# A linear-attention and MLP kernel: k's column maxima by way of DRAM instead of TensorE

## The chip, the cores and the metric

The kernel runs on one core of a Trainium2 chip. The metric is the device time of one execution in microseconds (us); the time before is the median of three runs. Beside it stands one profiled execution, from whose trace all rows below are taken.

A core has five engines with an instruction queue each: TensorE (PE in the rows, its weight loads PEld), VectorE (DVE), ScalarE (ACT), GpSimd (POOL) and SyncE (SP), which here only issues DMAs. An instruction waits at the head of its queue until the semaphores that it needs are set, and everything behind it waits too.

## The reference

```python
q_s = softmax over the 64 columns of each row of q          # with the row's maximum subtracted
k_s = k - np.max(k, axis=2, keepdims=True)                  # maximum over the 576 positions
k_s = np.exp(k_s)
k_s = k_s / (np.sum(k_s, axis=2, keepdims=True) + 1e-09)
kv  = np.einsum('bhsd,bhse->bhde', k_s, v)
x   = np.einsum('bhsd,bhde->bhse', q_s, kv)                 # then 4608 rows x 512
h   = x @ w_in                                              # 512 x 2048
g   = 0 where h <= -1, h where h >= 1, else (h + 1)**2 / 4
out = g @ w_out                                             # 2048 x 512
```

There are 8 batches of 8 heads, 576 positions and 64 columns. The step that the change touches is `np.max(k, axis=2)`: for each column of k one maximum over all positions of its head.

## The kernel before, in words

Two heads make a pair, so a batch has 4 pairs with 128 columns each. The 4608 rows of x are cut into 9 chunks of 512 rows. For each chunk the MLP runs 16 times over 128 hidden columns: a first product `h` (line 1446), the activation on ACT and DVE (lines 1596 to 1605), and a second product `o` (line 1659). All operands are split into a high and a low part, so a product is three matmuls of 128x512. Chunks 0 to 2 are done one by one; chunks 3 to 8 go in twos with a scheme of seven products (`hA`, `hb`, `hC`, line 1505) in place of eight.

Between these matmuls stands the attention. For batches 0 and 1 k is loaded transposed (columns on the partitions, `in_kt`), where the maximum is a plain reduction along the row (line 952). For batches 2 to 7 k is loaded with positions on the partitions (128 partitions, 5 positions each, `in_k`), two pairs at a time, in the function `attention_two`. It is called twice for each of the six batches, 12 times in all. There the maximum goes these steps for the two pairs:

- `k_max` (line 1213, DVE): maximum over the 5 positions that one partition holds, read with a stride; 128x128 values per pair, into `m2`.
- `k_tr` (line 1221, PE): a transpose of `m2` into PSUM, bank `a`, one per pair.
- `k_top` (line 1227, DVE): the maximum of each row of the transposed tile, for both pairs, into `mx`.
- `k_spread` (line 1232, PE): a transpose of that column broadcast to 128 columns, so that every partition has all 128 maxima, in PSUM.
- `k_sub` (line 1242, DVE) subtracts it, `k_exp` (line 1248, ACT) takes the exponent, `kv_mms` (line 1258, PE) makes the 20 small matmuls of `kv` for the two pairs, each of which shows as two in the trace.

The order of all instructions is written out before the program is built. The class `Plan` holds every operation with an engine, a duration, a due time and what it depends on. `order`, `late` and `early` make a list of it; `settle` then tries changes, one for each number in the table `TURNS` (a seed of a random choice), and keeps a change where the mean of three plays (`play`) ends no later. So a change of any operation moves instructions on every engine of the whole program. SP has one queue for all DMAs, in that order; a store that waits for its data holds the loads behind it.

A ring (`ring(tag, n)`) stands for n buffers that are used in turn: who takes one waits for the last readers of the one n before it. PSUM bank `a` is such a ring of one, shared by the scaled weights (`sg`, line 603), `mt`, `kv` and half of `x`.

## Time and profile before

| | |
|---|---|
| median of 3 runs | 846.63 us (845.81 to 847.31) |
| profiled execution, its own time | 844.76 us |
| its span from the first to the last instruction | 843.0 us |
| PE busy | 828.4 us, 98% of the span |
| DVE, ACT, POOL busy | 457.3, 442.5, 329.1 us |
| TensorE clock granted | full speed (2.4 GHz) in every slice |
| DMA | 166.38 MB, mean 197 GB/s |

The page sums the whole program. PE is the engine to look at: a gap in it lengthens the run, unless it is made up later. A busy PE is not a PE at its peak, as matmuls overlap, so what a piece of PE work costs is read from the distance of the starts around it, not from its duration.

### The profile page before, as it was taken

How to read it: one execution, taken by the hardware profiler on the slowest of the kernel's cores; microseconds unless marked ns; L12 is line 12 of the kernel's file. 1: busy time of each engine (PE TensorE's matmuls, PEld its weight loads, DVE VectorE, ACT ScalarE, POOL GpSimd, SP SyncE). 2: the span in 40 equal slices, each digit the busy share in tenths (PEclk: the TensorE clock that was granted, in tenths of full speed). 3: DMA queues.
4: the chain of work that ended last, by engine and by line, in shares of the span. 5: the costliest groups of instructions: out<-in, count | busy, mean ns of one | idle time of the engine just before them, and what ended most of it. 6: DMA issues, size and time to landing. Idle time of an engine off the chain costs nothing.

```text
span 843.0 us, 12228 instructions
## 1 busy us (share of the span) xinstructions
PE 828.4 (98%) x4364; PEld 663.6 (79%) x4364; DVE 457.3 (54%) x853; ACT 442.5 (52%) x758; POOL 329.1 (39%) x291
## 2 busy tenths in 40 slices
PE   8899999999999999999999999999999999999998
PEld 6587778877777787877877888787778888888786
DVE  6887774566756656776754315765641034545300
ACT  6787756443466454644656445554574245444522
POOL 4664555552446756200217691102157600000153
PEclk9999999999999999999999999999999999999999
DMA  9898865457578566766675536556465254544232
GB/s 338 274 318 294 290 218 213 145 165 241 193 258 274 173 217 224 246 215 228 194 248 206 153 99 194 195 193 210 145 216 178 76 187 138 175 138 162 75 102 87
DMA packets 65580, 166.38 MB, mean 197 GB/s; under 512 B 7280, under 2 KB 7536, under 8 KB 65520
## 3 DMA queue, kind: packets, MB, share of 16 engines
q1 hardware_dynamic: 65520, 165.61, 58.7%
q8 instruction: 34, 0.56, 0.3%
q14 instruction: 26, 0.21, 0.1%
HBM read 122.06 MB, written 43.52 MB: 196 GB/s over the span
## 4 chain that ended last, share of the span: by engine, by line
PE 93%; DVE 2%; ACT 2%; issue 1%; POOL 1%; DMA 1%; POOLq 0%; ACTq 0%
PE o L1659 45%; PE h L1446 16%; PE hA L1505 15%; PE hC L1505 8%; PE hb L1505 4%; PE x L839 2%; PE kv L1258 2%; PE warm L1841 1%; PE kv L988 1%; DMA out<-osb 1%; DVE qmo L1345 0%; ACT r L1596 0%; PE ep L963 0%; ACT osb L533 0%; PE tp L1035 0%
## 5 line engine op out<-in xcount | busy, mean ns | idle before, releaser
L1659 PE MATMUL o<-wl,gh 128*128 128x512 f32 x576 | 227.8, 396 | 0.3 <-ACT osb L533 0.3
L1659 PE MATMUL o<-wh,gl 128*128 128x512 f32 x576 | 224.9, 390 | 0.1
L1659 PE MATMUL o<-wh,gh 128*128 128x512 f32 x576 | 224.4, 390 | 0.0
L1505 PE MATMUL hA<-x,w 128*128 128x512 f32 x576 | 145.8, 392 | 1.6 <-ACT sn_P L533 1.2
L1659 PEld LDWEIGHTS o<-wl,gh 128*128 128x128 f32 x576 | 108.1, 188 | 26.8 <-issue 3.6
L1659 PEld LDWEIGHTS o<-wh,gl 128*128 128x128 f32 x576 | 108.1, 188 | 24.9 <-POOL gl L1648 1.0
L1505 PEld LDWEIGHTS hA<-x,w 128*128 128x128 f32 x576 | 107.2, 188 | 26.0 <-ACT sn_P L533 1.8
L1659 PEld LDWEIGHTS o<-wh,gh 128*128 128x128 f32 x576 | 108.2, 188 | 21.4
L1446 PE MATMUL h<-x,w 128*128 128x512 f32 x432 | 110.1, 396 | 2.2 <-DVE gl L1648 1.5
L1446 PEld LDWEIGHTS h<-x,w 128*128 128x128 f32 x432 | 79.3, 188 | 23.0 <-DVE gl L1648 2.1
L1600 ACT ACTIVATE r<-r 128x512 f32<-128x512 f32 x139 | 87.8, 633 | 3.8
L1505 PE MATMUL hC<-x,w 128*128 128x512 f32 x288 | 73.9, 392 | 0.1
L1596 ACT ACTIVATE r<-c,half 128x512 f32<-128x512 f32 x48 | 34.7, 723 | 68.2 <-DVE c L1529 68.1
L1648 POOL TENSOR_TENSOR gl<-gs,gh 128x512 fp32r<-128x512 f32 x42 | 54.2, 1291 | 41.7 <-ACT gh L1643 41.1
L1354 POOL TENSOR_TENSOR q<-q,qzb 128x512 f32<-128x512 f32 x28 | 28.9, 1050 | 105.3 <-DVE qzb L1376 91.0
L1354 POOL TENSOR_TENSOR q<-q,qmb 128x512 f32<-128x512 f32 x28 | 28.8, 1049 | 100.9 <-DVE qmb L1346 100.9
L1154 POOL TENSOR_TENSOR x<-xc,x 128x512 fp32r<-128x512 f32 x40 | 51.8, 1307 | 35.9 <-ACT x L1149 35.9
L1643 ACT CAST gh<-gs 128x512 fp32r<-128x512 f32 x42 | 26.1, 622 | 73.2 <-PE o L1659 63.4
L1505 PEld LDWEIGHTS hC<-x,w 128*128 128x128 f32 x288 | 53.6, 188 | 12.3 <-DVE sn_P L535 0.5
L1596 ACT ACTIVATE r<-h,half 128x512 f32<-128x512 f32 x48 | 33.0, 687 | 52.2 <-PE h L1446 51.9
L1648 POOL TENSOR_TENSOR gl<-c,gh 128x512 fp32r<-128x512 f32 x6 | 7.8, 1294 | 126.9 <-ACT gh L1643 126.8
L1605 DVE SCALAR_TENSOR_TENSOR h<-h,r 128x512 f32<-128x512 f32 x48 | 33.1, 694 | 37.1 <-ACT r L1600 34.0
(123 smaller groups left out, 1176.3 us busy)
## 6 DMA issues: line engine op xcount, KB each, us to landing
w<-b SPq DMA_DIRECT2D x50, 512.0 KB, 4.5
w<-s SPq DMA_DIRECT2D x48, 512.0 KB, 3.5
st<-in_w SPq DMA_DIRECT2D x32, 512.0 KB, 6.2
g<-c SPq DMA_DIRECT2D x42, 256.0 KB, 4.1
gs<-g SPq DMA_DIRECT2D x42, 256.0 KB, 2.6
v<-in_v SPq DMA_DIRECT2D x32, 325.0 KB, 4.9
q<-in_q SPq DMA_DIRECT2D x36, 256.0 KB, 3.7
out<-osb SPq DMA_DIRECT2D x35, 256.0 KB, 2.5
```

The lines of the kernel that those rows point to most:

```text
L839: nc.tensor.matmul(t[r][cols, :, p0:p1], kvt[rows, g % NKV, pr, :], q[pr]["tq"][rows, :, p0:p1], start=True, stop=True, tile_position=(r * ...
L1154: eng.tensor_tensor(x[:, 1, :], t["xc"][:, at, :], f32(x[:, 0, :]), ALU.subtract)
L1258: nc.tensor.matmul(kv[d, i, :], t[pr]["k"][:, j, d], t[pr]["v"][:, j, e * (D + 1) : (e + 1) * (D + 1)], start=(j == 0), stop=(j == KJ - 1) ...
L1354: nc.gpsimd.tensor_tensor(qf, qf, at, alu)
L1446: nc.tensor.matmul(t["h"], lhs, rhs, start=(turn == 0 and i == 0), stop=(turn == NPAIR - 1 and i == 2),)
L1505: nc.tensor.matmul(banks[b]["h"], lhs, rhs, start=(begins and not kk and not m), stop=(ends and kk == 1 and m == 2), skip_group_check=True,)
L1596: nc.scalar.activation(t["r"], t["h"], AF.Relu, bias=half[:, :1], scale=0.5)
L1600: nc.scalar.activation(t["r"], t["r"], AF.Square)
L1605: nc.vector.scalar_tensor_tensor(t["h"], t["h"], 1.0, t["r"], ALU.max, ALU.min)
L1643: nc.scalar.copy(t["gh"], t["h"])
L1648: eng.tensor_tensor(t["gl"], t["h"], f32(t["gh"]), ALU.subtract)
L1659: nc.tensor.matmul(outs[c, j], lhs[:, s], rhs, start=(begins and i == 0), stop=(closes and i == 2),)
```

## The change

For batches 2 to 7 the transposed copy of k is now loaded as well (`in_kt` holds all 8 batches, 24 more loads of 288 KB), into the buffers from which k itself follows later. `k_max` is the plain reduction along the row, one column of a fixed tile `kmax` per pair. `m_turn` turns that tile by blocks of 32x32 on DVE, so that the maxima of a pair lie in 4 partitions of 32 values. `m_store` writes them to DRAM, 4 rows of 128 bytes, one DMA per pair; `m_load` reads both pairs' 256 values back to all 128 partitions, one DMA of 128 KB. `k_sub` reads that tile from SBUF. `k_tr`, `k_top` and `k_spread` are gone: 48 transposes on PE, of some 3900 matmul instructions written there before, and 12 reductions on DVE. Chains of this kind run 12 times, as before.

The planner's `play` now adds 0.1 to an operation on PE of another mode than the one before (0 for the big matmuls, 1 for `x`, 2 for `kv`, 3 for transposes), two durations of PE operations are 0.09 and 0.1 lower, and the table `TURNS` is another. The maxima's operations have due times of their own.

```diff
--- before.py
+++ after.py
@@ -91,6 +91,7 @@
         self.store = False
         self.margin = 0.8 if kb else 0.0
         self.wire = kb / 330
+        self.mode = 0
         for d in deps:
             d.users.append(self)
 
@@ -122,76 +123,66 @@
     UNDER_WAY = 8
 
     TURNS = (
-        10001, 10002, 10003, 10011, 10013, 10026, 10029, 10031, 10033, 10036, 10041, 10042,
...
+        6, 9, 10, 15, 19, 20, 25, 27, 30, 31, 37, 39, 41, 42, 43, 44, 45, 46, 47, 49, 57, 58,
...
     )
 
     CASES, LATE = 3, 1.6
@@ -321,6 +312,7 @@
         free = dict.fromkeys(("PE", "ACT", "DVE", "POOL", "SP", "port", "wire"), 0.0)
         last = dict.fromkeys(free)
         ends, gaps, why = {}, [], {}
+        mode = 0
         for op in order:
             e = op.engine
             t, by = free[e], last[e]
@@ -349,6 +341,8 @@
                 gaps.append((op, t - free[e]))
                 if t > free[e] + 3 and t > START:
                     t += 2.4
+            if e == "PE" and op.mode != mode:
+                t, mode = t + 0.1, op.mode
             ends[op] = free[e] = t + op.us
             if op.port:
                 free["port"], last["port"] = ends[op], op
@@ -535,6 +529,7 @@
             nc.vector.tensor_copy(out, src)
 
     half = const.tile([P, 32], F32, name="half")
+    kmax = const.tile([P, 64], F32, name="kmax")
 
     kvt = const.tile([P, NKV, NPAIR, D], F32, name="kvt")
     early = ExitStack()
@@ -878,7 +873,8 @@
         rings_ = [ring(f"ps {tag}", 1) for _, tag in banks]
         deps = [kvdone.get((b, pr)) for b in (c - 1, c) for pr in two]
         deps = [d for d in deps if d] + [d for r in rings_ for d in r.wait()]
-        xm = do("PE", 1.05, due, x_mm, *ready, *deps)
+        xm = do("PE", 0.95, due, x_mm, *ready, *deps)
+        xm.mode = 1
         for i, pr in enumerate(two):
             ring(f"wk t{'ab'[i]}", 2).free(xm)
             kvread[c - 1, pr] = xm
@@ -1050,6 +1046,7 @@
         rrz.take(kz)
         et = ring(f"ps h{pr % 2}", 1) if first else rpk
         tr = do("PE", 0.6, 2, kt_tr, ke, *rpk.wait(), *(et.wait() * first))
+        tr.mode = 3
         rpk.take(tr)
         copies = [("DVE", 0.69, False)], [("ACT", 0.25, False)]
         kc = do("ACT", 0.58, 2.5, kt_copy, tr, *rk.wait(), other=copies[0])
@@ -1057,12 +1054,14 @@
         if not first:
             rpk.free(kc)
             tr = do("PE", 0.25, 2.7, kt_tr2, ke, *rpk.wait())
+            tr.mode = 3
             rk.free(tr)
         et.take(tr)
         kd = do("DVE", 0.25, 2.8, kt_tail, tr, kc, other=copies[1])
         et.free(kd)
         deps = [kc, kd, lv, *(rpk.wait() if not first else [])]
         mm = do("PE", 0.9, 3.5, kv_mm, *deps)
+        mm.mode = 2
         if not first:
             rpk.take(mm)
         rk.free(mm)
@@ -1082,6 +1081,7 @@
         qn = do("POOL", 1.04, 3, q_rows("qrz", ALU.mult), qz, port=True)
         rqz.free(qn)
         tr = do("PE", 0.45, 3.6, q_tr, qn, *rpq.wait())
+        tr.mode = 3
         rpq.take(tr)
         rq.free(tr)
         if first:
@@ -1207,38 +1207,34 @@
 
         def k_max(i):
             def emit():
-                if not i:
-                    b["m"] = wk.tile([P, 2, P], F32, tag="m2", name=f"m2_{n}")
-                k = t[two[i]]["k"].rearrange("p j d -> p d j")
-                nc.vector.tensor_reduce(b["m"][:, i, :], k, AX.X, ALU.max)
-
-            return emit
-
-        def k_tr(i):
-            def emit():
-                if not i:
-                    b["mt"] = ps_a.tile([P, 4, P], F32, tag="a", name=f"mt_{n}")
-                nc.tensor.transpose(b["mt"][:, i, :], b["m"][:, i, :], ident)
-
-            return emit
-
-        def k_top():
-            b["mx"] = sm.tile([P, 32], F32, tag="mx", name=f"mx_{n}", bufs=1)
-            nc.vector.tensor_reduce(b["mx"][:, :2], b["mt"][:, 0:2, :], AX.X, ALU.max)
-
-        def k_spread(i):
-            def emit():
-                t[two[i]]["mb"] = b["mt"][:, 2 + i, :]
-                nc.tensor.transpose(
-                    t[two[i]]["mb"], b["mx"][:, i : i + 1].broadcast_to([P, P]), ident
+                kt_ = t[two[i]]["kt"].rearrange("p j s -> p (j s)")
+                nc.vector.tensor_reduce(kmax[:, i : i + 1], kt_, AX.X, ALU.max)
+
+            return emit
+
+        def m_turn():
+            b["mt"] = sm.tile([P, QB], F32, tag="mt", name=f"mt_{n}", bufs=1)
+            nc.vector.transpose(b["mt"], kmax[:, :QB])
+
+        def m_store(i):
+            def emit():
+                nc.sync.dma_start(
+                    maxima[i].rearrange("(r p) -> r p", p=QB), b["mt"][i : P : QB, :]
                 )
 
             return emit
 
+        def m_load():
+            b["m"] = wk.tile([P, 2, P], F32, tag="m2", name=f"m2_{n}")
+            nc.sync.dma_start(
+                b["m"].rearrange("p i d -> p (i d)"),
+                maxima.rearrange("i p -> (i p)").unsqueeze(0).broadcast_to([P, 2 * P]),
+            )
+
         def k_sub(pr):
             def emit():
                 k = t[pr]["k"]
-                mb = t[pr]["mb"].unsqueeze(1).broadcast_to([P, KJ, P])
+                mb = b["m"][:, pr % 2, :].unsqueeze(1).broadcast_to([P, KJ, P])
                 nc.vector.tensor_tensor(k, k, mb, ALU.subtract)
 
             return emit
@@ -1276,37 +1272,42 @@
             )
 
         if c < NB:
-            rm = ring("wk m2", 1)
-            loads, rooms, maxed = {}, {}, rm.wait()
+            loads, rooms = {}, {}
+            tag = ("k", "st1")[h]
+            maxima = dp.tile([2, P], F32, name=f"mk{n}")
+            rx, ry, rm = ring("sm mx", 1), ring("sm mt", 1), ring("wk m2", 1)
+            tops, before = [], rx.wait()
             for i, pr in enumerate(two):
-                tag = ("k", "st1")[h]
-                loads[pr, "k"], rooms[pr, "k"] = load(
-                    pr, "k", k[c - KT, pr], [P, KJ, P], 320, kdue + 6 * i, tag
+                lk, rk = load(pr, "kt", kt[c, pr], [P, 1, S], 288, kdue - 14 + 3 * i, tag)
+                km = do("DVE", 0.75, kdue - 12 + 3 * i, k_max(i), lk, *before)
+                rk.free(km)
+                tops.append(km)
+                if not i:
+                    rx.take(km)
+                before = [km]
+            turn = do("DVE", 0.15, kdue - 7, m_turn, *tops, *ry.wait(), port=True)
+            rx.free(turn)
+            ry.take(turn)
+            kept = [plan.save(0.45, kdue - 6, m_store(i), [turn], 32) for i in range(2)]
+            ry.free(*kept)
+            spread = plan.read(0.45, kdue - 2, m_load, [*kept, *rm.wait()], 128)
+            rm.take(spread)
+            subs, exps = [], []
+            for i, pr in enumerate(two):
+                lk, rooms[pr, "k"] = load(
+                    pr, "k", k[c - KT, pr], [P, KJ, P], 320, kdue + 10 + 6 * i, tag
                 )
                 loads[pr, "v"], rooms[pr, "v"] = load(
                     pr, "v", v[c, pr], [P, KJ, P + 2], 325, kdue + 33 + 3 * i, "v"
                 )
-            for i, pr in enumerate(two):
-                km = do("DVE", 1.3, kdue + 6 * i, k_max(i), loads[pr, "k"], *maxed, port=True)
-                maxed = [km]
-                if not i:
-                    rm.take(km)
-                loads[pr, "m"] = km
-            exps = []
-            ra = ring("ps a", 1)
-            one = do("PE", 0.13, kdue + 8, k_tr(0), loads[two[0], "m"], *ra.wait())
-            ra.take(one)
-            other = do("PE", 0.13, kdue + 8, k_tr(1), loads[two[1], "m"], one)
-            top = do("DVE", 0.4, kdue + 10, k_top, one, other)
-            rm.free(top)
-            spread = [do("PE", 0.13, kdue + 12, k_spread(i), top) for i in range(2)]
-            subs = [do("DVE", 0.81, kdue + 14, k_sub(pr), *spread) for pr in two]
-            ra.free(*subs)
+                subs.append(do("DVE", 0.9, kdue + 14, k_sub(pr), lk, spread, port=True))
+            rm.free(*subs)
             exps = [do("ACT", 0.74, kdue + 20 + 12 * i, k_exp(pr), subs[i]) for i, pr in enumerate(two)]
             ra = ring("ps a", 1)
             at = kdue + 34
             deps = [loads[pr, "v"] for pr in two]
-            mm = do("PE", 1.34, at, kv_mms, *exps, *deps, *ra.wait())
+            mm = do("PE", 1.25, at, kv_mms, *exps, *deps, *ra.wait())
+            mm.mode = 2
             ra.take(mm)
             for pr in two:
                 rooms[pr, "k"].free(mm)
@@ -1831,6 +1832,7 @@
     stream.__enter__()
     make_identity(nc, ident)
     nc.vector.memset(half, 0.5)
+    nc.gpsimd.memset(kmax, 0.0)
 
     nc.scalar.activation(half[:, 1:2], half[:, :1], AF.Exp)
 
@@ -1869,7 +1871,7 @@
 
     kk = rows(inputs["k"]).transpose(0, 1, 3, 4, 2, 5).reshape(b, NPAIR, P, 2 * KJ * D)
 
-    kt = rows(inputs["k"])[:KT].transpose(0, 1, 2, 5, 4, 3).reshape(KT, NPAIR, P, KJ * P)
+    kt = rows(inputs["k"]).transpose(0, 1, 2, 5, 4, 3).reshape(b, NPAIR, P, KJ * P)
     kt = kt[..., :S]
     kk = kk[KT:]
     vv = rows(inputs["v"], pad=True)
```

How instructions moved is shown at three places. The names give batch (or chunk) and pair (or hidden block), and a buffer number last.

The first is PE at the start: the first two blocks of the first layer (`h_0_0`, `h_0_1`, twelve matmuls each, three per part of x) and the transposes of batch 1's k (`ep`, then `et`, which takes the same bank after DVE has copied `ep` out). Before:

```order
L1446 MATMUL h_0_0_473<-x2_482,w_0_0_454 128x512 x3
L1446 MATMUL h_0_1_501<-x2_482,x10_488 128x512 x3
L1446 MATMUL h_0_0_473<-x3_491,w_0_0_454 128x512 x3
L963 MATMUL ep_1_0_538<-ident_95,k_1_0_410 128x128 x4
L1446 MATMUL h_0_1_501<-x3_491,x10_488 128x512 x3
L972 MATMUL et_1_0_570<-ident_95,k_1_0_410 64x128
L1659 MATMUL o_0_1_572<-wl0_97,gh_0_0_562 128x512
```

After:

```order
L1447 MATMUL h_0_0_498<-x3_502,w_0_0_469 128x512 x3
L1447 MATMUL h_0_1_523<-x1_463,x10_487 128x512 x3
L1447 MATMUL h_0_1_523<-x2_495,x10_487 128x512 x3
L1447 MATMUL h_0_1_523<-x3_502,x10_487 128x512 x3
L959 MATMUL ep_1_0_557<-ident_96,k_1_0_419 128x128 x4
L968 MATMUL et_1_0_581<-ident_96,k_1_0_419 64x128
L1660 MATMUL o_0_0_583<-wl0_98,gh_0_0_573 128x512
```

Between the end of `h_0_0` and `et` there are now nine matmuls instead of three.

The second is ACT before the `kv` products of batch 4's first two pairs; `r` and `gh` are the activation of a hidden block of chunk 1, of which block 15 is the last. Before:

```order
L1596 ACTIVATE r_1_14_2426<-h_1_14_2343,half_93 128x512
L1600 ACTIVATE r_1_14_2426<-r_1_14_2426 128x512
L1596 ACTIVATE r_1_15_2445<-h_1_15_2396,half_93 128x512
L1600 ACTIVATE r_1_15_2445<-r_1_15_2445 128x512
L1248 ACTIVATE k_4_1_2216<-k_4_1_2216 128x640
L1248 ACTIVATE k_4_0_2214<-k_4_0_2214 128x640
L1643 CAST gh_1_14_2464<-h_1_14_2343 128x512
```

After:

```order
L1597 ACTIVATE r_1_13_2350<-h_1_13_2280,half_93 128x512
L1601 ACTIVATE r_1_13_2350<-r_1_13_2350 128x512
L1644 CAST gh_1_12_2379<-h_1_12_2255 128x512
L1244 ACTIVATE k_4_0_2261<-k_4_0_2261 128x640
L1644 CAST gh_1_13_2402<-h_1_13_2280 128x512
L1244 ACTIVATE k_4_1_2284<-k_4_1_2284 128x640
L849 CAST x12_2441<-x_2_1_0_2423 128x512
L849 CAST x13_2448<-x_2_1_1_2424 128x512
L1597 ACTIVATE r_1_14_2455<-h_1_14_2398,half_93 128x512
```

Both exponents of k now stand ahead of the activation of block 14; they stood behind that of block 15.

The third is DVE, and SP beside it, at the maxima of batch 3's pairs 2 and 3 (`mt_3_1` is the turned tile, `m2_3_1` what is read back). On DVE before, with batch 4's first pairs between:

```order
L1227 TENSOR_REDUCE mx_4_0_2428<-mt_4_0_2408 128x2
L1213 TENSOR_REDUCE m2_3_1_2433<-k_3_2_2000 128x128
L1213 TENSOR_REDUCE m2_3_1_2433<-k_3_3_2010 128x128
L1242 TENSOR_TENSOR k_4_1_2216<-k_4_1_2216,mt_4_0_2408 128x640
L1242 TENSOR_TENSOR k_4_0_2214<-k_4_0_2214,mt_4_0_2408 128x640
```

On DVE after:

```order
L1217 STREAM_TRANSPOSE mt_3_1_2337<-kmax_94 128x32
L1649 TENSOR_TENSOR gl_1_11_2354<-h_1_11_2237,gh_1_11_2344 128x512
L1382 STREAM_TRANSPOSE ta_3_0_2361<-q_3_0_2107 128x512
L1606 SCALAR_TENSOR_TENSOR h_1_13_2280<-h_1_13_2280,r_1_13_2350 128x512
L1238 TENSOR_TENSOR k_4_0_2261<-k_4_0_2261,m2_4_0_2314 128x640
L1238 TENSOR_TENSOR k_4_1_2284<-k_4_1_2284,m2_4_0_2314 128x640
L1649 TENSOR_TENSOR gl_1_12_2388<-h_1_12_2255,gh_1_12_2379 128x512
L1382 STREAM_TRANSPOSE tb_3_1_2396<-q_3_1_2142 128x512
L1649 TENSOR_TENSOR gl_1_13_2410<-h_1_13_2280,gh_1_13_2402 128x512
L1335 TENSOR_REDUCE qa_4_0_2421<-q_4_0_2368 128x16
L1238 TENSOR_TENSOR k_3_2_2292<-k_3_2_2292,m2_3_1_2390 128x640
```

On SP after:

```order
L1221 DMA mk3_1_167<-mt_3_1_2337 4x32 x2
L671 DMA w_2_0_2352<-b0_113 128x1024
L671 DMA w_2_1_2356<-b1_114 128x1024
L1201 DMA q_4_0_2368<-in_q 128x512
L671 DMA w_2_2_2373<-b2_115 128x1024
L1229 DMA m2_3_1_2390<-mk3_1_167 128x256
```

Between the turn and the first subtraction that needs its maxima stand nine other instructions of DVE; between the two stores and the load stand four loads of SP. Over the 12 round trips the instructions of DVE in between are 13, 17, 19, 14, 9, 23, 13, 10, 19, 17, 18 and 50.

## Rows read from the trace of the kernel before

**Rows 1.** The page: busy us, share of the span, instructions.

```profile
PE 828.4 (98%) x4364; PEld 663.6 (79%) x4364; DVE 457.3 (54%) x853; ACT 442.5 (52%) x758; POOL 329.1 (39%) x291
```

**Rows 2.** Timeline of PE, 122.2 to 123.5 us: start us, length us, instruction.

```profile
122.02 0.84 PE L1446 MATMUL h<-x,x 128*128 128x512 f32 x3
122.70 0.38 PE L1232 MATMUL mt<-ident,mx 128*128 128x128 f32 x2
122.84 0.48 PE L1659 MATMUL o<-wl,gh 128*128 128x512 f32 x1
123.15 0.40 PE L1659 MATMUL o<-wh,gh 128*128 128x512 f32 x1
```

**Rows 3.** Timeline of PE, 127.4 to 130.3 us.

```profile
128.20 0.39 PE L1659 MATMUL o<-wh,gl 128*128 128x512 f32 x1
128.52 1.39 PE L1258 MATMUL kv<-v,k 128*64 128x65 f32 x40
129.84 0.50 PE L1659 MATMUL o<-wl,gh 128*128 128x512 f32 x1
130.18 0.39 PE L1659 MATMUL o<-wh,gh 128*128 128x512 f32 x1
```

**Rows 4.** Timeline of PE at 214, 233 and 334 us; in brackets idle, releaser.

```profile
215.04 0.39 PE L1659 MATMUL o<-wh,gl 128*128 128x512 f32 x1
216.08 1.39 PE L1258 MATMUL kv<-v,k 128*64 128x65 f32 x40 [0.66 <-ACT k L1248]
...
232.96 1.39 PE L1258 MATMUL kv<-v,k 128*64 128x65 f32 x40
235.87 0.50 PE L1446 MATMUL h<-x,w 128*128 128x512 f32 x1 [1.53 <-DVE gl L1648]
...
333.62 1.42 PE L1258 MATMUL kv<-v,k 128*64 128x65 f32 x40 [0.28 <-ACT k L1248]
336.22 1.45 PE L1505 MATMUL hA<-x,w 128*128 128x512 f32 x5 [1.19 <-ACT sn_P L533]
```

**Rows 5.** Timeline of ACT, 212 to 216.5 us.

```profile
213.42 0.69 ACT L1596 ACTIVATE r<-h,half 128x512 f32<-128x512 f32 x1 [0.93 <-PE h L1446]
214.15 0.63 ACT L1600 ACTIVATE r<-r 128x512 f32<-128x512 f32 x1
214.69 1.34 ACT L1248 ACTIVATE k<-k 128x640 f32<-128x640 f32 x2
```

**Rows 6.** Timeline of PE, 20 to 34 us.

```profile
28.58 0.94 PE L1446 MATMUL h<-x,x 128*128 128x512 f32 x3
31.61 0.30 PE L972 MATMUL et<-ident,k 128*64 128x128 f32 x1 [2.09 <-DVE k L535]
```

**Rows 7.** Groups by line: busy us, mean ns | idle before, releasers.

```profile
L1648 DVE TENSOR_TENSOR gl<-h,gh 128x512 fp32r<-128x512 f32 x48 | 33.1, 689 | 22.1 <-ACT gh L1643 21.3
...
L1213 DVE TENSOR_REDUCE m<-k 128x128 f32<-128x640 f32 x24 | 30.8, 1302 | 0.0
...
L1242 DVE TENSOR_TENSOR k<-k,mt 128x640 f32<-128x640 f32 x24 | 18.7, 815 | 13.5 <-PE mt L1232 13.5
...
L1227 DVE TENSOR_REDUCE mx<-mt 128x2 f32<-128x256 f32 x12 | 5.1, 421 | 10.0 <-PE mt L1221 10.0
L1221 PE MATMUL mt<-ident,m 128*128 128x128 f32 x24 | 4.9, 271 | 0.0
...
L952 DVE TENSOR_REDUCE nm<-k 128x1 f32<-128x576 f32 x4 | 3.0, 746 | 0.9 <-DMA k<-in_kt 0.9
```

**Rows 8.** DMA issues: count, KB each, median us from issue to landing.

```profile
gs<-g SPq DMA_DIRECT2D x42, 256.0 KB, 2.6
k<-in_k SPq DMA_DIRECT2D x24, 320.0 KB, 4.7
b<-w SPq DMA_DIRECT2D x10, 512.0 KB, 6.9
```

**Rows 9.** Windows, 100 to 560 us: busy us by engine, clock, DMA share, GB/s.

```profile
100.00:560.00 460.00, 455.69 (x2531) 364.49 (x2530) 278.28 (x533) 239.84 (x410) 201.07 (x182) 1.00 0.61 206
```

128 rows, old and new, of the table TURNS are left out of this document.

## The prediction

> **What bounds the kernel now.** First the page's busy table: PE is busy 828.4 us, 98% of the span, and no other engine is over 54% [rows 1]. So the time can fall in two ways only: PE gets less work, or its few gaps close. Second, the timeline of PE, read by starts. In the stream of big matmuls three starts fill 122.02 to 122.70, 0.227 us each [rows 2]; whatever makes the distance of two starts longer than that is the cost of what stands between. Third, the same timeline where PE stood idle, with the releaser in brackets [rows 4, 6], and the queue of the engine that released it [rows 5].
>
> **Term 1, the transposes that go.** A pair of them starts at 122.70, where the next matmul would have started. That matmul starts at 122.84 and the one after it at 123.15, where an unbroken stream would have 122.93 [rows 2]. So a pair costs 0.22 us of PE's stream, although each of its instructions lasts 271 ns [rows 7]: most of that lies over its neighbours. The order has 24 pairs (48 transposes, a few of them standing alone; I give one alone half a pair). All of it lies on the engine that bounds: 24 x 0.22 = 5.3 us less. The duration is the other end: 48 x 0.271 = 13.0 us. I take the starts, since these are what the next matmul waits for.
> The page "TensorE: Matmul & The Clock Gate" of the Trainium skill, Part 4, says that a 128x128 transpose in a kernel's context takes about 275 ns. The trace's duration agrees; taken as the price it would make this term 13.2 us (an estimate by that page), and the distance of the starts in this trace speaks against it.
>
> **Term 2, the gaps at the `kv` products.** An undisturbed visit to `kv` starts 0.32 us after the last matmul, and the next matmul 1.32 us after it [rows 3]. Three of the 12 visits are longer [rows 4]. At 216 us `kv` starts 1.04 us after the matmul, 0.72 too late: it waits for the exponents, and ACT had them behind the activation of the last block of chunk 1, whose relu began at 213.42 when PE had finished that block; 0.69 and 0.63 us of activation, then two exponents [rows 5]. At 233 us the matmul behind `kv` starts 2.91 us after it, 1.59 too late: it is the first of a hidden block and waits for DVE to free a PSUM bank. At 334 us it starts 2.60 after, 1.28 too late, on an ACT copy that stood behind the exponents and four other ACT instructions, and `kv` itself idled 0.28. Sum 0.72 + 1.59 + 1.56 = 3.9 us.
> In the new order the exponents of the first of these stand before the activation of block 14, so they no longer wait for block 15. At the other two the matmuls right behind `kv` are second-layer products of blocks that are done, not the start of a bank that has to be freed. So all three gaps should close. But what is late next is not known for every visit: the first `kv` of batch 2 now follows its subtractions and exponents closely (in the order the exponents stand right behind the activation of chunk 0's block 15), so I give back 0.9 us and take 3.0. The bounds are 3.9, and a loss of 4 us if as many new gaps open elsewhere as close here.
>
> **Term 3, the start.** `et` starts at 31.61 after idling 2.09 us on a DVE copy [rows 6]. That copy stands on DVE behind the activation of `h_0_0`. In the new order PE has nine matmuls instead of three between the end of `h_0_0` and `et`, 6 x 0.227 = 1.4 us more cover. Against it, the squaring of that block moves from POOL to ACT behind a cast and a scaling, three instructions of 0.63 to 0.69 like those in [rows 5], about 1.9 us in place of one squaring on POOL. No row here shows POOL's; between ACT's 0.63 and the whole 1.9 it makes the copy 0 to 1.3 us later, and I take 0.9. That leaves 0.5 us of gain. The bounds: the whole 2.1 gained, or 1.5 lost, since the loads at the start are in another order too; that is as much as the cover won. The clearing of `kmax` on POOL stands before any load has landed and costs nothing.
>
> **What costs nothing.** DVE: 24 strided reductions of 1.302 us become 24 plain ones of the length 576, 0.746 us as in the same reduction of batch 1, and 12 of 0.421 go [rows 7]: 13.3 + 5.1 = 18.4 us less. Added are 12 turns of a 32-wide tile, which no row shows; they lie between nothing and the 0.421 of the reduction they replace, and I take 0.15, 1.8 us. The subtraction from SBUF in place of PSUM may differ from 0.815 either way; 10% of it would be 2 us in all. DVE works 278 of 460 us in this stage [rows 9], so some 15 us less there moves the end only through waits, which terms 2 and 3 hold. The steps that vanish were also waits: DVE idled 10.0 us before `k_top` and 13.5 before `k_sub` [rows 7], in a chain with slack.
> DMA: 24 x 288 KB and 12 x 128 KB are 8.65 MB more. Between 100 and 560 us that is 19 GB/s on top of 206, and the share of 0.61 would become 0.67 [rows 9]. The work that hides it is PE's; the SP queue loads several us ahead of use.
>
> **The added wait.** Each round trip is a turn, two stores, a load that waits for both, and a subtraction that waits for the load, with everything behind it on DVE: `gl` and the activation's last step, for which PE waits. The shortest room is nine instructions of DVE, two of them subtractions of 0.815 and seven of 512 columns, each about 0.69 as `gl` [rows 7]: 6.5 us even if DVE never idles. Ten instructions at batch 6 make about the same, 13 and 14 make 8 to 9, and the others 10.4 and more, by the same durations. The trip itself: nearest rows 2.6 us for 256 KB read back from DRAM and, at the far end, 6.9 us for a 512 KB store of the weights and 4.7 for a 320 KB load [rows 8]. I take 2.6 twice, as these are small transfers, 5.2 us: just inside the shortest room. The far end is 11.6 us.
> [...]
>
> **The sum.** The profiled execution lasts 844.76 us. 844.76 - 5.3 - 3.0 - 0.5 = 835.96. The median of the runs lies 1.87 us over that execution (846.63), so the forecast for the median is 837.8 us.
>
> **Rivals.**
> - A: only the transposes go. The gaps at `kv` close, and others open, since every engine's order is new; the start does the same. For it: gaps of before were single places in an order, not a law of the kernel. Against it: the exponents stand well ahead in nearly all of the 12 visits now. 846.63 - 5.3 = 841.3 us.
> - B: all known gaps close. 5.3 + 3.9 + 2.1 = 11.3: 835.3 us. For it: DVE and ACT have more air. Against: other chains at the start end at nearly the same time.
> - C, slower: the round trip. At 11.6 us it overruns rooms of 6.5 (twice), 8 (twice), 9, and some between 10 and 11 by 5.1 + 5.1 + 3.6 + 3.6 + 2.6 + 1.2 + 1.0 + 0.9 = 23 us of DVE standing still; if half of it reaches PE, 11.6 us are lost against 8.8 gained: 849.4 us. It decides from about 10.5 us a trip on. Against it: the 12 trips lie in a stage with a DMA share of 0.61 [rows 9], and the 6.9 us are of the ten stores of the weights in chunk 0, before it.
> - D: the change does what it says, but the loads of the copy hold SP's queue (its stores wait for the turn, its load for the stores, and the loads of the weights stand behind), and PE loses about what it gains: 846.6 us, for which some 9 us of new gaps are needed.
>
> **Chances.** The forecast (836 to 840 us) 0.50; A (840 to 844.5) 0.24; B (under 836) 0.11; C 0.08; D 0.07. A measurement of this kernel tells 0.2%, 1.7 us, from no change. All of the forecast, A and B, and a little of D are faster by more than that: 0.86. Within it falls most of D: 0.05. Slower: C and the rest of D, 0.09. The range is 833.0 to 845.0 us: down past B's case by a little more than a measurement can tell, and up over A to where D begins; it leaves out C, most of D and a little below B.
>
> **What would show it.** PE should have no `mt` rows, 48 matmul instructions fewer, and a busy time that falls by about 5 us. The rows around `kv` should show 0.32 and 1.32 us in all 12 visits. `et` should idle under 2 us. DVE should be busy some 15 us less. The subtraction of k should idle little before it; if it waits for a DMA at many of the 12 places, and `gl` or `h` are late behind it, C is right. If the `kv` gaps are closed but PE idles elsewhere as long, A is. It is wrong altogether if PE's starts in the stream are no longer 0.227 apart.

## The result, and the profile after

The changed kernel takes 837.66 us (median of 5 runs, 835.96 to 840.43) against 845.81 us (844.84 to 847.31) for the kernel before on the same chip: a ratio of 0.9908, 95% interval 0.9884 to 0.9933. It is 8.15 us faster by the medians, and lies 0.14 us from the forecast (837.8 us). Its profiled execution lasts 839.19 us (span 837.4), 5.57 us less than that of before, where the forecast's sum had 8.8 us less.

The busy table of its page, which answers to [rows 1]: busy us, share of the span, instructions.

```profile
PE 823.3 (98%) x4316; PEld 660.8 (79%) x4316; DVE 454.5 (54%) x860; ACT 442.0 (53%) x752; POOL 335.6 (40%) x291
```

PE has 48 instructions less and 5.1 us less to do. DVE, which was to lose some 15 us, lost 2.8.

The timeline of PE around the first `kv` product of batch 2, the place of the first gap in [rows 4]:

```profile
214.71 0.39 PE L1660 MATMUL o<-wh,gl 128*128 128x512 f32 x1
215.02 1.39 PE L1254 MATMUL kv<-v,k 128*64 128x65 f32 x40
216.34 3.02 PE L1447 MATMUL h<-x,w 128*128 128x512 f32 x12
```

0.31 us ahead and 1.32 behind are the undisturbed distances of [rows 3], and all 12 visits look like this now. The same timeline at the start and in the weights' stage, which answers to [rows 6]; in brackets idle time and releaser:

```profile
22.82 3.59 PE L1447 MATMUL h<-x,w 128*128 128x512 f32 x9 [2.34 <-DVE x L856]
...
31.90 0.30 PE L968 MATMUL et<-ident,k 128*64 128x128 f32 x1 [1.30 <-DVE k L529]
...
72.19 2.12 PE L1447 MATMUL h<-x,w 128*128 128x512 f32 x8 [1.96 <-DVE gl L1649]
```

`et` idles 0.8 us less than in [rows 6], but two gaps of 2 us are new. Three groups of DVE (busy us, mean ns | idle before), which answer to [rows 7], and the window of [rows 9]:

```profile
L1238 DVE TENSOR_TENSOR k<-k,m 128x640 f32<-128x640 f32 x24 | 26.5, 1129 | 0.8 <-DMA m<-mk 0.7
...
L1211 DVE TENSOR_REDUCE kmax<-kt 128x1 f32<-128x576 f32 x24 | 17.5, 741 | 1.1 <-DMA kt<-in_kt 0.9
...
L1217 DVE STREAM_TRANSPOSE mt<-kmax 128x32 f32<-128x32 f32 x12 | 2.4, 201 | 0.2
```

```profile
100.00:560.00 460.00, 459.77 (x2565) 369.85 (x2563) 284.22 (x557) 246.18 (x417) 209.96 (x184) 1.00 0.68 230
```

In these 460 us PE stands still for 0.23. The DMA share of 0.68 and the 230 GB/s are near what the prediction worked out (0.67 and 225).

**Where the time went.** I took the start of each of the 3312 matmuls of 512 columns on PE's timeline, subtracted 0.227 us from each distance to the next, and summed what is left by what stands between the two: transposes, `kv` products, the products `x` with the transposes of q (`tp`), or nothing. "Again" is the changed kernel's second profiled execution (first experiment), "no pairs" the kernel before without its transposes.

| us | before | no pairs | changed | again |
|---|---|---|---|---|
| first such start | 20.65 | 20.99 | 22.82 | 22.86 |
| transposes of the maxima | 3.11 | 0 | 0 | 0 |
| `kv` products | 24.75 | 24.91 | 20.87 | 20.77 |
| nothing, start 10 to 120 ns late | 9.31 | 7.41 | 6.58 | 6.34 |
| nothing, under 10 ns late | 1.30 | 0.84 | 0.68 | 0.62 |
| nothing, over 120 ns late | 4.92 | 6.25 | 7.58 | 5.89 |
| `ep`, `et` | 3.91 | 4.59 | 3.50 | 3.16 |
| `tp`, `x` | 19.30 | 19.30 | 19.29 | 19.28 |
| last such start | 838.83 | 835.88 | 832.91 | 830.52 |

The transposes and the late starts take 6.5 us with them (lines 2, 4 and 5; 6.8 in "again"), the `kv` products 3.9 (4.0). The start and gaps in the stream give back 2.2 and 2.7 in this execution, 2.2 and 1.0 in the other.

### The profile page after: what moved, and what is told of

It is laid out like the page before. It is cut to its first block, busy times and chain, and to the rows that moved or that the text cites. A ratio compares the mean times of both kernels' runs of the same rounds, so it can differ in the third digit from the quotient of the medians.

```text
span 837.4 us, 12261 instructions
## 1 busy us (share of the span) xinstructions
PE 823.3 (98%) x4316; PEld 660.8 (79%) x4316; DVE 454.5 (54%) x860; ACT 442.0 (53%) x752; POOL 335.6 (40%) x291
## 4 chain that ended last, share of the span: by engine, by line
PE 90%; DMA 4%; DVE 2%; ACT 1%; issue 1%; POOL 1%; SPq 0%; POOLq 0%; DVEq 0%; ACTq 0%
PE o L1660 44%; PE hA L1506 16%; PE h L1447 13%; PE hC L1506 8%; PE hb L1506 4%; DMA st<-in_w 3%; PE x L834 2%; PE kv L1254 2%; DMA kt<-in_kt 1%; DMA out<-osb 1%; POOL wl L633 0%; PE kv L984 0%; DVE st L603 0%; ACT r L1597 0%; PE tp L1031 0%
## 5 line engine op out<-in xcount | busy, mean ns | idle before, releaser
L1154 POOL TENSOR_TENSOR x<-xc,x 128x512 fp32r<-128x512 f32 x42 | 53.8, 1295 | 40.2 <-ACT x L1149 40.2
L1355 POOL TENSOR_TENSOR q<-q,qzb 128x512 f32<-128x512 f32 x28 | 30.9, 1124 | 86.4 <-DVE qzb L1377 64.5
L1644 ACT CAST gh<-gs 128x512 fp32r<-128x512 f32 x42 | 26.1, 622 | 72.3 <-PE o L1660 70.4
L1355 POOL TENSOR_TENSOR q<-q,qmb 128x512 f32<-128x512 f32 x28 | 31.4, 1139 | 78.5 <-DVE qmb L1347 74.4
L1603 POOL TENSOR_TENSOR r<-r 128x512 f32<-128x512 f32 x4 | 4.2, 1042 | 120.9 <-ACT r L1597 120.9
```

What stands on the lines that cost most here:

```text
L1154: eng.tensor_tensor(x[:, 1, :], t["xc"][:, at, :], f32(x[:, 0, :]), ALU.subtract)
L1355: nc.gpsimd.tensor_tensor(qf, qf, at, alu)
L1644: nc.scalar.copy(t["gh"], t["h"])
```

## The experiments

Each kernel was timed beside the kernel before on the same chip, in 4 to 12 executions; the ratio is to that one, in brackets its 95% interval.

**The changed kernel again**, without an edit.

> The changed kernel again, unchanged: which of its losses before 110 us belong to its order and which to one execution. Theory: the late start is the order's (PE's first big matmul at 22.8 us after some 2.3 us idle on the DVE subtraction of x that stands behind two shifts, then starts 427 ns apart to about 27 us), and comes again to within 0.3 us. The 2.1 us gap at 72 us followed a load of the weights that took 7.8 us to land, so it belongs to that execution and should differ by over 1 us. Rival: that gap is the order's too and comes again with 2 us. Time 837.7, 836 to 840.

Measured: 836.85 us, ratio 0.9888 (0.9875 to 0.9902). The start came again (22.86 us, idle 2.34), and so did the gap in the weights' stage, 2.48 us at 70.45 us: it is the order's, and the theory on it falls. What did not come again was the slow stretch behind the start. The windows 24 to 32 us of the first and of this execution (clock, DMA share and GB/s last):

```profile
24.00:32.00 8.00, 6.70 (x26) 5.16 (x25) 4.96 (x11) 5.52 (x12) 3.50 (x3) 0.81 0.73 280
```

```profile
24.00:32.00 8.00, 6.72 (x32) 5.15 (x31) 6.47 (x13) 6.53 (x13) 4.17 (x4) 1.00 0.91 313
```

After the same idle time the granted clock was at the lower of its two levels, 1.2 GHz, for a part of the first window (starts 427 ns apart from 23.6 to 27.0 us), and at 2.4 GHz in the whole of the second. The 25th matmul, the first one behind `et`, started at 32.01 and at 30.43 us: 1.6 us apart in one and the same kernel.

**One instruction at the start moved**

```diff
     order = plan.settle()
+    low = xdone[0, 0]                    # DVE's subtraction of x that PE waits for at 22.8 us
+    order.remove(low)
+    cast = order.index(low.deps[0])
+    behind = [i for i in range(cast, len(order)) if order[i].engine == "DVE"]
+    order.insert(behind[1], low)
```

> The changed kernel with one DVE instruction moved: the first block's subtraction of x (line 856) ahead of the two shifts of weights that it stood behind. Theory: PE's first big matmul starts at about 21.2 instead of 22.8 us, PE idles 0.7 instead of 2.3 us ahead of it, and the stretch at half clock goes, so the start is 1.6 to 3.2 us earlier and most of it stays: 835 us (834.5 to 836). Rival: the two shifts come 0.7 us later, so the weights of the next blocks are late, and the stage up to 110 us, which is bound by the chain from load over DVE to PE, takes it all back: 837.7.

In the changed kernel, DVE's queue was this at that place:

```profile
20.51 1.66 DVE L603 TENSOR_SCALAR st<-st 128x512 uint32<-128x512 uint32 x2
22.09 0.68 DVE L856 TENSOR_TENSOR x<-x,x 128x512 fp32r<-128x512 f32 x1
```

Measured: 839.32 us, 0.9914 (0.9895 to 0.9933): no gain. PE's timeline:

```profile
20.89 1.65 PE L1447 MATMUL h<-x,w 128*128 128x512 f32 x6 [0.76 <-DVE x L856]
24.54 0.96 PE L1447 MATMUL h<-x,w 128*128 128x512 f32 x3 [1.99 <-DVE x L856]
```

PE starts 1.9 us earlier and stops six matmuls later for the next head pair's x. Neither theory had this: one wait gave way to the next of the same kind. At the 25th matmul (30.75 us) this kernel is 0.3 us behind "again". Later it loses more in this execution: behind the gap in the weights' stage, 2.78 us at 70.60 us, the granted clock was low (0.83 from 66 to 76 us).

**24 pairs of transposes put back**

```diff
                 if begins:
                     bank(b)
+                if name == "P1":
+                    for i in range(2):
+                        nc.tensor.transpose(banks[b]["h"][:, i * P : (i + 1) * P], ident, ident)
```

> The changed kernel with 24 pairs of transposes put back into PE's stream (two 128x128 transposes of the identity ahead of the first product P1 of each hidden pair of blocks, into the bank that this product then overwrites); nothing waits for them beyond the next matmul. Theory (the price is the distance of the starts, 0.22 us a pair): 5.3 us more than the changed kernel, 843.0. Rival (the price is the duration, 0.271 us for each): 13 us more, 850.7. Second rival: P1 starts behind a wait for its bank at some places, so a pair is partly hidden: under 3 us more.

Measured: 843.24 us (840.93 to 847.27), 0.9964 (0.995 to 0.9979), 6.4 us above the changed kernel on the same chip. On PE's timeline a pair starts at 332.50, and the matmul behind it 0.13 us later:

```profile
331.00 1.65 PE L1509 MATMUL hA<-x,w 128*128 128x512 f32 x6
332.50 0.38 PE L1502 MATMUL hA<-ident 128*128 128x128 f32 x2
332.63 1.64 PE L1509 MATMUL hA<-x,w 128*128 128x512 f32 x6
```

By the starts, taken to the second matmul behind a pair, the 24 pairs cost 0.225 to 0.232 us each, 5.47 us. The price is the distance; the duration (13 us) and the hidden pair (under 3 us) are refuted.

**The kernel before without its transposes**

```diff
-                nc.tensor.transpose(b["mt"][:, i, :], b["m"][:, i, :], ident)
+                pass
...
-            nc.vector.tensor_reduce(b["mx"][:, :2], b["mt"][:, 0:2, :], AX.X, ALU.max)
...
-                t[two[i]]["mb"] = b["mt"][:, 2 + i, :]
-                nc.tensor.transpose(...)
+                t[two[i]]["mb"] = ident
```

> The kernel before with its order kept and the maxima's transposes left out: neither pair is issued, the 12 short reductions between them are left out, and k has the identity subtracted out of SBUF (so it leaves out the maxima of batches 2 to 7; the strided reductions still run). Theory (two separate gains): only the 24 pairs' 0.228 us go, 5.5 us, and the three gaps at the kv products stay: 840.4 us (839.5 to 841.5). Rival (the gaps hung on the transposes, since k's subtraction waited for PE): the gaps close here too, 836 to 838.5, and the new order gave nothing.

Measured: 841.32 us, 0.9942 (0.9928 to 0.9956), 4.7 us less than before (3.7 to 6.1). The three gaps are where they were; its rows on PE at two of the places of [rows 4]:

```profile
216.39 1.39 PE L1253 MATMUL kv<-v,k 128*64 128x65 f32 x40 [0.66 <-ACT k L1243]
...
235.78 1.43 PE L1441 MATMUL h<-x,w 128*128 128x512 f32 x5 [1.53 <-DVE gl L1643]
```

So the two gains are separate: the transposes, and the gaps that belonged to the order. In its one profiled execution the start, `et` and the stream's gaps give back 2.5 of the 5.5 us, so that it lies 2.95 us under the profiled one of before, where the medians differ by 4.7.

**The planner's part alone, in the kernel before**

```diff
+            if e == "PE" and op.mode != mode:
+                t, mode = t + 0.1, op.mode
             ends[op] = free[e] = t + op.us
```

with the modes and the durations 0.95 and 1.25 as in the change, and the list of turns of before.

> The kernel before with the planner's part of the change alone: 0.1 us for each change of TensorE's mode, 0.95 and 1.25 us for the x and kv products, with its own list of turns. Its order comes out new throughout. Theory: counting the modes does not itself take work or waits away; a list of turns that was found for other costs gives an order that is no better, 845 to 849. Rival: the count makes the planner see PE's time rightly and closes the gaps at the kv products by itself, 841 to 843.

Measured: 847.69 us, 1.0022 (1.0009 to 1.0034). The count of the modes brings nothing by itself. Of the long visits to `kv` one is left, at 236 us, 2.27 us over an undisturbed one, so two closed without the new chain; but other gaps opened. Another order has other gaps. Which part of the change, the new costs, the new list of turns or the chain, made the order in which all three are closed is not shown.

**The new chain left out**

```diff
-    kmax = const.tile([P, 64], F32, name="kmax")
+    kmax = const.tile([P, 2 * P], F32, name="kmax")       # zeros, subtracted in place of m
...                                                         # no kt load, maximum, turn, store, load
```

> The changed kernel without the new chain: no second copy of k is loaded, no maxima, no turn, no stores to DRAM and no load back; k has zeros subtracted from it out of SBUF, with the same instruction. It leaves out the maxima of batches 2 to 7, with all else in the same order. Theory (the chain is hidden behind PE): the same time within 1.7 us, 836 to 839.4. Rival (its loads and trips cost PE several us that the gain covers): 3 to 5 us faster, 833 to 834.5.

Measured: 842.98 us, 0.9967 (0.9954 to 0.998): 6.1 us above "again" on the same chip, which neither theory had. By the account of the starts there was no new gap; 232 starts of the stream were 10 to 120 ns late in place of 62, and more were a few ns late. These two lines of the table come to 12.4 us in place of 7.0, nearly the whole loss, and the larger part of it (3.5 us) is in the starts under 10 ns. The next two kernels asked why.

> The changed kernel with one constant made larger and nothing else: kmax is 256 instead of 64 columns wide, of which the same 64 are used. All that is allocated behind it in SBUF moves up by 768 bytes a partition; no instruction, no order and no data differ. In the kernel without the chain the same constant was 256 columns wide, and its PE stream had 232 starts that were 10 to 120 ns late instead of 62, most of them in the second layer. Theory (the addresses did that): the same slips here, 841 to 844 us. Rival (the addresses do nothing, and it was the missing chain): 836 to 838.5, with some 60 such starts.

> The changed kernel without the new chain once more (no second copy of k, no maxima, no turn, no stores, no load back; zeros are subtracted, so it leaves out the maxima of batches 2 to 7), now with every tile at the address that it has in the changed kernel. If the addresses made the first such kernel slow: 836 to 838.5 us, as the changed kernel, since the chain is hidden; if the chain costs something and the addresses hid it: under 835. Rival: 841 to 844 again, so the missing chain itself slows PE's stream in some way.

The larger constant alone: 838.60 us, 0.9914 (0.9901 to 0.9928), 65 late starts. The missing chain with every tile in its place: 838.40 us, 0.9909 (0.9894 to 0.9924), 67 late starts. Both are the changed kernel's time. So the chain as such is hidden. Why the first kernel lost some 6 us stays open: it differs from the last in the places of its tiles (those behind the dropped `m` tile lie lower, which the larger constant alone doesn't do) and in one clearing.

**Every round trip doubled**

```diff
+            nc.sync.dma_start(second.rearrange("i p -> (i p)").unsqueeze(0), b["m"][:1].rearrange("p i d -> p (i d)"))
+            nc.sync.dma_start(b["m"]..., second...broadcast_to([P, 2 * P]))
```

> The changed kernel with every round trip doubled: behind the load back, the row is stored to DRAM a second time and loaded again, on the same queue, so SP waits for the load, then for the store, and the subtraction of k waits for the second load. By the trace of the changed kernel a subtraction waited for its load once, 0.7 us. Theory (the rooms on DVE and the copies in front of it cover a second trip of some 5 us in most of the 12 places): under 3 us more, 837 to 840. Rival (a trip of about 10 us is what the prediction took as the point from which DVE's waits decide, and SP's queue is held for as long): 843 to 850, with k's subtraction waiting at five or more places.

Measured: 866.88 us, 1.025 (1.0236 to 1.0264). The rival's mechanism holds, with seven waits of k's subtraction, and the time lies far above both ranges. The list of waits (us, times, longest), then DVE and PE at the first of the trips:

```profile
DVE k L1243 <- DMA m<-ml: 32.8, 7, 12.0
```

```profile
106.44 0.21 DVE L1217 STREAM_TRANSPOSE mt<-kmax 128x32 f32<-128x32 f32 x1
...
121.75 1.56 DVE L1243 TENSOR_TENSOR k<-k,m 128x640 f32<-128x640 f32 x2 [3.91 <-DMA m<-ml]
...
128.68 1.56 PE L1453 MATMUL h<-x,w 128*128 128x512 f32 x4 [2.94 <-DVE gl L1655]
```

32.8 us of DVE standing still became 24.8 us at PE's last matmul, against "again", in the profiled execution of 861.55 us; by the medians it is some 28 us over the kernels with the changed kernel's time on the same chip (838.40 and 838.60). About 4 of the 24.8 us are TensorE's clock: behind PE's waits, at 129, 225 and 269 us, the granted clock fell to the lower level, and 20 starts are 427 ns apart in place of 227. This kernel also shows what its single trips take, since its second store leaves SP's queue when the first load has landed. At the first trip:

```profile
106.68 1.15 SPq L1221 DMA_DIRECT2D mk<-mt  x2
...
112.87 0.33 SPq L1229 DMA_DIRECT2D m<-mk  x1
115.80 0.25 SPq L1233 DMA_DIRECT2D ml<-m  x1
```

From the end of the turn (106.65) to 115.80 are 9.2 us, of which the load's own way is 2.9. Over the 12 trips it is 6.2 to 17.9 us, median 12.4; the load's way 2.9 to 5.9, median 4.0; the rest is spent on SP's queue, behind other transfers and the stores' landing. The second trips hold that queue too: the load back leaves it 2.6 to 14.1 us after the turn here (median 7.8), and 2.6 to 11.4 us in the changed kernel (median 5.9).

**Block 6 ahead of a shift of weights**

```diff
+    def ahead(op, other):                # op goes right before other in the order
+        order.remove(op)
+        order.insert(order.index(other), op)
+
+    one, cast, low = steps[0, 6]         # h, gh and gl of block 6
+    shift = [o for o in order[: order.index(one)] if o.engine == "DVE"][-1]
+    for o in (one, cast, low):
+        ahead(o, shift)
```

In the execution "again", DVE's queue ahead of PE's gap at 70.45 us was this: the last step of block 6's activation stands behind a shift, which waits for its load.

```profile
67.34 1.11 DVE L603 TENSOR_SCALAR st<-st 128x512 uint32<-128x512 uint32 x1 [1.59 <-DMA st<-in_w]
68.37 1.28 DVE L1606 SCALAR_TENSOR_TENSOR h<-h,r 128x512 f32<-128x512 f32 x2
69.70 0.69 DVE L1649 TENSOR_TENSOR gl<-h,gh 128x512 fp32r<-128x512 f32 x1
```

> The changed kernel with three instructions of chunk 0's block 6 moved ahead of one shift of weights (line 603) that waits for its load: the last step of the activation and gl on DVE, and the cast gh on ACT between them. In the two runs of the changed kernel PE idled 2.0 and 2.5 us at 70 to 72 us for that gl. Theory: the gap shrinks to under 0.5 us, the shift had been waiting anyway, and the time falls by 1.5 to 2.5 us: 835 (834.3 to 836). Rival: that stage is bound by the loads of the weights, so PE waits as long a block or two later: 837 to 838.

Measured: 837.62 us, 0.9904 (0.9889 to 0.9918). That gap is gone, and PE stops 0.60 us behind the next nine matmuls:

```profile
69.40 2.35 PE L1447 MATMUL h<-x,w 128*128 128x512 f32 x9
72.35 0.97 PE L1447 MATMUL h<-x,x 128*128 128x512 f32 x3 [0.60 <-DVE gl L1650]
```

In its profiled execution the clock was low again at the start (0.85 from 24 to 32 us, 1.0 us behind "again" at the 25th matmul), and at the 192nd matmul it was 0.15 us ahead. So some 1.1 us were won between the two, too little for the medians to show.

**Both pieces moved**, the start's with the third head pair as well:

```diff
+    one, two = xdone[0, 0], xdone[0, 2]
+    begin = order.index(one.deps[0])
+    shift = [o for o in order[begin:] if o.engine == "DVE"][1]
+    for o in (one, two.deps[0], two):
+        ahead(o, shift)
```

> The changed kernel with two pieces of order moved: the three instructions of block 6 as in the run before, and at the start the casts and subtractions of x for the first and the third head pair (ACT line 849, DVE line 856) ahead of the weights' cast and shifts. With the first alone PE waited at 24.5 us for the third, so nothing was won. Theory: both are there in time, PE starts at about 21 us without a second stop over 1 us and stays at full clock, 1.5 to 2.5 us are won and kept: 835 us (833.5 to 836.2). Rival: the weights' cast and shifts, 1.4 us later, make PE wait for the weights of blocks 1 and 2 for as long: 837 to 838.6.

Measured: 836.13 us (834.91 to 838.34), 0.9888 (0.987 to 0.9906). The lowest median of all, but the ratio is that of "again" (0.9888): not shown to be better than the changed kernel. PE still stops a second time at the start, 1.47 us at 25.45 us for a later subtraction of x; the gap at 70 us is 0.37.

**POOL's work on q left out**

```diff
         def q_rows(i, what, alu):
             def emit():
-                nc.gpsimd.tensor_tensor(qf, qf, at, alu)
+                pass
```

> The changed kernel without POOL's subtractions and products on q in chunks 2 to 8 (line 1346's function): it leaves out q's maxima and division there, all else is in the same order. In the changed kernel k's subtraction takes 0.82 us with POOL idle and up to 1.90 us beside such an instruction, 26.5 us in 24. Theory (DVE and POOL hinder each other with two operands in SBUF): k's subtraction falls to 20 to 21 us in all, and the time stays within 1.7 us, since DVE does not bound. Rival (the new DMA traffic makes it slow): it stays at 25 us or more.

Measured: 838.03 us, 0.9906 (0.989 to 0.9921): the time stays. k's subtraction falls to 23.7 us from 26.8 in "again" (the same order). That speaks against the rival, but it is not the 20 to 21 of the theory: 5 of the 24 still lie wholly beside another POOL instruction (9 before).

## Why the prediction was right

**Term 1, the transposes (5.3 us): right.** Pairs put back cost 5.47 us by the starts, taken out of the kernel before 5.5 (lines 2, 4 and 5 of the table). The account of the changed kernel has 6.5; that the further 1.0 us of late starts hung on the transposes is not shown.

**Term 2, the gaps at `kv` (3.0 of 3.9 us): right in place, short by 0.9.** All three closed. The kernel without transposes kept them, so they were the order's, as the term said; that the new chain is not needed for them to stay closed shows in the kernel without it, whose 12 visits are undisturbed too. The loss for "what is late next" was rightly expected and wrongly placed: it did not come at `kv`.

**Term 3, the start (0.5 us gained): wrong as a step.** `et` behaved as forecast (1.30 us idle, under 2), but the term looked at this one place. The first big matmul comes 2.2 us later, behind two shifts of weights on DVE, and at 70 us there is a gap of 2 to 2.5 us that was nowhere in the sum. From the first matmul to the 25th the kernel gains 1.9 to 3.5 us against before, so that by then it stands between 0.3 us behind and 1.3 ahead, depending on the clock; by the 288th, at 103 to 105 us, it is 3.8 to 5.5 us behind. About 1.0 us of that is a `kv` visit that now comes before it and is no loss; of the rest, the gap at 70 us is the largest single part. This is rival A's mechanism, in the weights' stage: gaps close at `kv` and others open. It did not decide, because terms 1 and 2 brought 10.3 us (10.7 in "again") in place of 8.3.

So the total is right in part because errors cancel, and that it is met to 0.14 us is luck. By the starts 10.3 us were won and 4.4 given back by the lines of the start, of the stream's gaps and of `et` (in "again" 10.7 and 2.4), against 8.8 forecast: the profiled execution was to fall to 835.96 us and fell to 839.19. The sum then added 1.87 us, since the median before lay that much over its profiled execution; the median of the changed kernel lies 1.53 us under its own. The two misses, 3.2 and 3.4 us, cancel. The kernel's runs scatter over 4.5 us.

**The added wait: right in outcome, both numbers wrong.** The trip was put at 5.2 us and the shortest room at 6.5. In the changed kernel the load back leaves SP's queue 2.6 to 11.4 us after the turn's end; with the 2.9 to 5.9 us that it takes in the kernel with doubled trips, a trip is 5.5 us at the least, an estimate, and over 10.5 at five places. The term left out the time on the queue. The rooms, from the turn's end to where DVE is free for the subtraction, are 9.0 us and more (median 13.8), since DVE waits for others in between; it also has more instructions there than were counted at some places, 20, 25 and 29 where 17, 19 and 23 were. The list of waits of the changed kernel:

```profile
DVE k L1238 <- DMA m<-mk: 0.7, 1, 0.7
```

That single wait is at the shortest room, in the timeline of DVE:

```profile
198.20 0.20 DVE L1217 STREAM_TRANSPOSE mt<-kmax 128x32 f32<-128x32 f32 x1
...
208.07 2.41 DVE L1238 TENSOR_TENSOR k<-k,m 128x640 f32<-128x640 f32 x2 [0.66 <-DMA m<-mk]
```

From the turn's end (198.40) to 207.41, where DVE was free, are 9.0 us; the trip took 9.7. Rival C did not happen, though its condition did: from about 10.5 us a trip on, it said, DVE's waits decide, but behind the five trips of that length DVE waited 0.04 us at most, as the rooms there are 11.3 us and more. What it had wrong were the rooms. Its mechanism shows where the trips are doubled: there 24.8 of DVE's 32.8 us reach PE, more than the half that it allowed. Rival D, SP's queue, shows in that kernel only: 3.3 us of PE's gaps were released by loads of weights, and in the changed kernel none.

**DVE's 15 us: wrong.** The reductions are as forecast (741 ns, 0.746 said; the turn 0.20, 0.15 said). k's subtraction grew by 7.8 us instead of "10%, 2 us", and the new order put six more evictions and five more scalings of `kv` on DVE, 4.0 and 1.3 us. Little hung on it: the kernel without POOL's work, with 3.1 us less in that subtraction, takes the same time.

## What to carry to other kernels

Price an instruction on the bounding engine by what it adds to the distance of the starts around it, not by its duration: 0.23 us a pair here, against 0.54. For a round trip through DRAM, add the time that its stores and load spend on the issuing queue, and measure the room in time on the waiting engine; one trip in each place is hidden here but for a wait of 0.7 us, and two cost 25. And a new order of a whole program opens gaps where the old one had none: look for them where other work stands in a queue ahead of what the bounding engine waits for, as the shifts of weights do at the start and at 70 us here, not only at the places that the change aims at.

## What was not expected

**DVE beside POOL.** The subtraction's duration by source (min/median/max ns), of the kernel before with the maxima in PSUM, and of the changed one with them in SBUF:

```profile
L1242 DVE TENSOR_TENSOR k<-k,mt x24: 803/815/822, 123.4 to 548.8; 128x640 f32<-128x640 f32 x24
```

```profile
L1238 DVE TENSOR_TENSOR k<-k,m x24: 761/884/1904, 120.4 to 530.7; 128x640 f32<-128x640 f32 x24
```

From PSUM it took 815 ns also in the 7 cases that lay wholly beside a POOL instruction. From SBUF it took 811 alone ("again", 9 cases) and 937 to 1909 beside one (9 cases), and POOL's instruction grew as well (of its last products on q the five that overlap such a subtraction last 1451 to 1631 ns in "again", the 23 others 1051 on average). In the kernel without transposes, which has the operand in SBUF but none of the new transfers, it took 26.1 us too: it is not the DMA. The Trainium skill, page "SBUF — State Buffer", section "Who interferes with whom", says that a DVE instruction with two inputs in SBUF and a GpSimd instruction that reads SBUF contend for a shared port, and one with a single SBUF input, outside DVE's two-port modes, does not. The traces agree in both halves, and the prediction should have used it.

**The clock after one and the same idle time.** PE idles 2.33 or 2.34 us ahead of its first big matmul in both profiled executions of the changed kernel and in seven of its variants. The granted clock of the next microseconds was at the lower level in six of these nine (0.81 from 24 to 32 us in the first) and at full speed in three (1.00 in "again"). The gap at 70 us was followed by the lower level in two kernels (2.78 us in the one with the start moved, 2.55 in the one without POOL's work) and by full speed after 2.48 us in "again". What decides between the two is not shown. The difference at the start is 1.6 us; whether it makes up a part of the 4.5 us over which this kernel's runs scatter is not shown either, as the mean granted clock of those five runs is 0.997 or 0.998 in all.
